# Strassen's seven quarter products for the second matrix product of an attention and feed-forward kernel

## The chip, the cores and the metric

The kernel runs on one core of a Trainium2 chip. The metric is the time of the program on the device in microseconds; the median of three runs of the kernel before is 319.86 us (319.72 to 320.0). The profile is of one execution, with a span of 317.4 us from its first to its last instruction.

The engines are named as in the profile: PE is TensorE (its weight loads are PEld), DVE is VectorE, ACT is ScalarE, POOL is GpSimd, SP is SyncE, which issues the stores. Each works through its own instructions in the order of the program.

## The reference, cut to what matters

```python
# q, k, v: (8 batches, 8 heads, 576 tokens, 64) float32; g_norm: (64,)
kv  = einsum('bhsd,bhse->bhde', k, v)
out = einsum('bhsd,bhde->bhse', q, kv)
rms = sqrt(mean(out * out, axis=-1, keepdims=True) + 1e-06)
out = out / rms * g_norm

x = out.transpose(0, 2, 1, 3).reshape(4608, 512)
h = x @ w_in                                  # w_in (512, 2048)
g = maximum(h, 0) + alpha * minimum(h, 0)     # alpha (2048,)
y = g @ w_out                                 # w_out (2048, 512), result float32
```

Linear attention without a softmax, a norm for each head, and a feed-forward part of two matrix products with a leaky activation between them.

## The kernel before

The 4608 tokens are worked on in nine blocks of W = 512 columns, numbered 0 to 8. For a block w the kernel makes `xt` (the normed attention output, features on the partitions), then 16 groups of the first product, `h_ps`, each 128 of the 2048 inner features by 512 tokens; each group leaves PSUM through ScalarE and VectorE as a tile `gt`. The second product takes `gt` as stationary operand, 128 tokens at a time, and sums 16 matmuls into a bank `y`.

```python
def ssq_mm(w, j):                       # norm of a pair of heads
    ot_ps, sq = ots.pop((w, j))
    ssq_ps = ps_q.tile([P, W], FP32, name="ssq_ps", tag="q")
    nc.tensor.matmul(out=ssq_ps[:], lhsT=mask16[:], rhs=sq[:], start=True, stop=True)
    rstd = attn_p.tile([P, W], FP32, name="rstd")
    nc.scalar.activation(out=rstd[:], in_=ssq_ps[:], func=AF.Ln, bias=eps_t[:], scale=inv_d)
    nc.scalar.activation(out=rstd[:], in_=rstd[:], func=AF.Exp, bias=0.0, scale=-0.5)
    ...
def m1_mm(h_ps, w, g, cs):              # first product: 4 matmuls of 512 columns a group
    for c in cs:
        nc.tensor.matmul(out=h_ps[:], lhsT=w_in_blk(c, g), rhs=xts[w, c][:], ...)

def m1_evac(h_ps, w, g):
    m_sb = gt_p.tile([P, W], FP32, name="m_sb", bufs=3)
    nc.scalar.activation(out=m_sb[:], in_=h_ps[:], func=AF.Relu, scale=-1.0)
    gt = gt_p.tile([P, W], FP16, name="gt", tag=f"gt{g}")
    nc.vector.scalar_tensor_tensor(out=gt[:], in0=m_sb[:], scalar=beta_sb[:, g : g + 1],
                                   in1=h_ps[:], op0=ALU.mult, op1=ALU.add)

def y_mm(y, w, a, g):                   # second product: 64 matmuls of 512 columns a block
    nc.tensor.matmul(out=y[:], lhsT=gts[w, g][:, a * P : (a + 1) * P], rhs=w_out_blk(g), ...)
```

The inputs of a batch (576 tokens) are loaded through Pool's queue and, for k and q, regrouped by a copy on Pool. The stage buffers are double.

```python
def load_batch(b, names=("k", "v", "q")):
    for nm in names:
        load_rem(b, nm)                 # nc.gpsimd.dma_start
        load_main(b, nm, 0, H)          # nc.gpsimd.dma_start into a stage tile (2 buffers)

def regroup_batch(b):
    for nm in ("k", "q"):
        regroup(b, nm, 0, H, nc.gpsimd) # a copy on Pool of 128x2048
```

The main loop runs the first product of block w together with the second product of block w - 1, and between the groups the attention steps of block w + 1 (`t` transposes q, `kv` makes k times v, `ot` multiplies both, `ssq` makes the norm and `xt`). The steps `t` and `kv` write one PSUM bank, `ssq` another.

```python
for w in range(1, NW):
    steps = window_steps(w + 1) if w + 1 < NW else []
    if 1 < w and w + 2 < B:
        load_batch(w + 2)
        regroup_batch(w + 2)
    for g in range(NF):                 # 16 groups
        if w == 1 and g == first_g - 1:
            load_batch(3)
            regroup_batch(3)
        m1_group(w, g)
        if w == 1:                      # the last quarter of block 0's second product
            y_mm(y, 0, AHEAD, g) ...
        else:                           # four matmuls of block w - 1's second product
            for gg in range(part * TPW, (part + 1) * TPW):
                y_mm(y, w - 1, a, gg)
            ...
        while steps and n - len(steps) < want:
            steps.pop(0)()
for a in range(TPW):                    # block 8's second product, with nothing beside it
    ...
```

PSUM has eight banks: three for `h_ps`, one for `y`, one for `t` and `kv`, two for `ot`, one for `ssq`.

Of the kernel before, what the change touches and what calls it, by code (L numbers as in the profile page):

```python
# [9 lines left out]
FP32 = mybir.dt.float32  # L10
FP16 = mybir.dt.float16
AF = mybir.ActivationFunctionType
# [5 lines left out]
def kernel(  # L18
# [11 lines left out]
    nc = tc.nc  # L30

    B, H, S, D = q.shape
    N_TOK, D_MODEL = out.shape
    D_FF = moe_w_in.shape[1]

    P = 128
    NPAIR = H // 2
    W = 512
    NW = N_TOK // W
    TPW = W // P  # L40
    TPP = S // P
    MAIN = TPP * P
    REM = S - MAIN
    NT = TPP + 1
    NF = D_FF // P
    NC = D_MODEL // P
    assert NC == NPAIR and 0 < REM < P
    inv_d = 1.0 / D

    const_p = ctx.enter_context(tc.tile_pool(name="constp", bufs=1))  # L50
    w_p = ctx.enter_context(tc.tile_pool(name="weights", bufs=1))
    xt_p = ctx.enter_context(tc.tile_pool(name="xt", bufs=3))
    qkv_p = ctx.enter_context(tc.tile_pool(name="qkv", bufs=1))
    stage_p = ctx.enter_context(tc.tile_pool(name="stage", bufs=2))
    attn_p = ctx.enter_context(tc.tile_pool(name="attn", bufs=2))
    gt_p = ctx.enter_context(tc.tile_pool(name="gt", bufs=2))
    ysb_p = ctx.enter_context(tc.tile_pool(name="ysb", bufs=4))
    ps_h = ctx.enter_context(tc.tile_pool(name="psh", bufs=3, space=bass.MemoryType.PSUM))
    ps_y = ctx.enter_context(tc.tile_pool(name="psy", bufs=1, space=bass.MemoryType.PSUM))
    ps_s = ctx.enter_context(tc.tile_pool(name="pss", bufs=1, space=bass.MemoryType.PSUM))  # L60
    ps_o = ctx.enter_context(tc.tile_pool(name="pso", bufs=2, space=bass.MemoryType.PSUM))
    ps_q = ctx.enter_context(tc.tile_pool(name="psq", bufs=1, space=bass.MemoryType.PSUM))
# [3 lines left out]
    )  # L66

    _set_id = list(get_activation_tables(nc.m.arch).keys()).index(
        "natural_log_exp_and_others"
    )  # L70
    nc.scalar.add_instruction(
        mybir.InstLoadActFuncSet(
            name=nc.get_next_instruction_name(),
# [18 lines left out]
    eps_t = const_p.tile([P, 1], FP32, name="eps_t")  # L92
# [5 lines left out]
    for nm, src in (("q", q), ("k", k), ("v", v)):  # L98
        rem0[nm] = ysb_p.tile([P, H, D], FP32, name=f"rem0{nm}", tag="y_sb")
        nc.sync.dma_start(  # L100
            out=rem0[nm][0:REM], in_=src[0, :, MAIN:S, :].rearrange("h s d -> s h d"),
# [12 lines left out]
    bufs = []  # L114
    for i in range(NBUF):
        t = {}
        for nm in ("k", "v", "q"):
            n = 1 if nm == "v" else NT
# [39 lines left out]
    WQ = 4  # L158
    w_in_sb = []
    w_out_sb = []  # L160
    FW = D_FF // WQ
    GW = NF // WQ
# [21 lines left out]
    def w_out_blk(g):  # L184
        i, r = divmod(g, GW)
        return w_out_sb[i][:, r, :]
# [14 lines left out]
    def keep_warm(n):  # L201
        ps = ps_s.tile([P, W], FP32, name="warm_ps", tag="s")
        for i in range(n):
            nc.tensor.matmul(out=ps[:], lhsT=mask16[:], rhs=warm16[:], start=True, stop=True)
# [4 lines left out]
        out=alpha_ps[:], lhsT=alpha_row[:], rhs=ident[0:NF, 0:NF], is_transpose=True,  # L209
        start=True, stop=True,  # L210
    )

    beta_sb = const_p.tile([P, NF], FP32, name="beta_sb")
    nc.vector.tensor_scalar(
        out=beta_sb[:], in0=alpha_ps[:], scalar1=-1.0, scalar2=1.0, op0=ALU.mult, op1=ALU.add,
# [42 lines left out]


    ots = {}  # L260

    def step_ot(w, j, pool=None):
        if pool is not None:
            ot_ps = pool[0].tile([P, W], FP32, name="ot_ps", tag=pool[1])
        else:
            ot_ps = ps_o.tile([P, W], FP32, name="ot_ps", tag="o")
        n0 = w * W
        while n0 < (w + 1) * W:
            b = n0 // S
            n1 = min((b + 1) * S, (w + 1) * W)  # L270
            nc.tensor.matmul(  # L271
                out=ot_ps[:, n0 - w * W : n1 - w * W], lhsT=kvs[b, j][:],
                rhs=qts[b, j][:, n0 - b * S : n1 - b * S], start=True, stop=True,
            )
            n0 = n1
        sq = attn_p.tile([P, W], FP16, name="sq_sb")
        nc.scalar.activation(out=sq[:], in_=ot_ps[:], func=AF.Square)  # L277
        ots[w, j] = (ot_ps, sq)
# [4 lines left out]

    def ssq_mm(w, j):
        ot_ps, sq = ots.pop((w, j))
        ssq_ps = ps_q.tile([P, W], FP32, name="ssq_ps", tag="q")
        nc.tensor.matmul(out=ssq_ps[:], lhsT=mask16[:], rhs=sq[:], start=True, stop=True)  # L287
        rstd = attn_p.tile([P, W], FP32, name="rstd")
        nc.scalar.activation(  # L289
            out=rstd[:], in_=ssq_ps[:], func=AF.Ln, bias=eps_t[:], scale=inv_d,  # L290
        )
        nc.scalar.activation(out=rstd[:], in_=rstd[:], func=AF.Exp, bias=0.0, scale=-0.5)  # L292
        ots[w, j] = (ot_ps, rstd)

    def norm(w, j):
# [21 lines left out]


    gts = {}

    def m1_mm(h_ps, w, g, cs):
        for c in cs:
            nc.tensor.matmul(  # L323
                out=h_ps[:], lhsT=w_in_blk(c, g), rhs=xts[w, c][:],
                start=(c == 0), stop=(c == NC - 1),
            )

    def m1_evac(h_ps, w, g):
        m_sb = gt_p.tile([P, W], FP32, name="m_sb", bufs=3)
        nc.scalar.activation(out=m_sb[:], in_=h_ps[:], func=AF.Relu, scale=-1.0)  # L330
        gt = gt_p.tile([P, W], FP16, name="gt", tag=f"gt{g}")
        nc.vector.scalar_tensor_tensor(  # L332
            out=gt[:], in0=m_sb[:], scalar=beta_sb[:, g : g + 1], in1=h_ps[:],
            op0=ALU.mult, op1=ALU.add,
        )
        gts[w, g] = gt

    def m1_group(w, g):
        h_ps = ps_h.tile([P, W], FP32, name="h_ps", tag="h")
        m1_mm(h_ps, w, g, range(NC))  # L340
        m1_evac(h_ps, w, g)


    def y_mm(y, w, a, g):
        nc.tensor.matmul(  # L345
            out=y[:], lhsT=gts[w, g][:, a * P : (a + 1) * P], rhs=w_out_blk(g),
            start=(g == 0), stop=(g == NF - 1),
        )

    def y_out(y, w, a):  # L350
        y_sb = ysb_p.tile([P, D_MODEL], FP32, name="y_sb")
        nc.scalar.copy(out=y_sb[:], in_=y[:])  # L352
        i = 0
        while i < P:
            b, r = divmod(w * W + a * P + i, S)
            if r < MAIN:
                t, p = divmod(r, P)
                cnt = min(P - i, P - p)
                rows = out[b * S : b * S + MAIN, :].rearrange("(p t) m -> t p m", t=TPP)
                dst = rows[t, p : p + cnt, :]  # L360
            else:
                cnt = min(P - i, S - r)
                dst = out[b * S + r : b * S + r + cnt, :]
            nc.sync.dma_start(out=dst, in_=y_sb[i : i + cnt, :])
            i += cnt


    H_POOL = (ps_h, "h")
    for nm in ("q", "k", "v"):
        nc.scalar.copy(out=bufs[0][nm][0:REM, 0 if nm == "v" else TPP, :, :], in_=rem0[nm][0:REM])  # L370
    regroup(0, "q", 0, H // 2)
    step_t(0, 0, H_POOL)
    regroup(0, "k", 0, H // 2)
    step_t(0, 1, H_POOL)
    keep_warm(3)
    step_kv(0, 0)
    step_kv(0, 1, H_POOL)
    step_ot(0, 0)
    step_ot(0, 1)
    regroup(0, "q", H // 2, H)  # L380
    step_t(0, 2, H_POOL)
    regroup(0, "k", H // 2, H)
    step_t(0, 3, H_POOL)
    ssq_mm(0, 0)
    ssq_mm(0, 1)
    norm(0, 0)
    step_kv(0, 2)
    step_kv(0, 3, H_POOL)
    norm(0, 1)
    step_ot(0, 2)  # L390
    step_ot(0, 3, (ps_y, "y"))
    first = [ps_h.tile([P, W], FP32, name="h_ps", tag="h") for g in range(3)]
    for g in range(3):
        m1_mm(first[g], 0, g, (0, 1))
    step_ssq(0, 2)
# [7 lines left out]
    for g in range(3, NF):  # L403
# [7 lines left out]
    AHEAD = 3  # L411
    ys = [
        ps_y.tile([P, W], FP32, name="ya", tag="y"),
        ps_h.tile([P, W], FP32, name="yb", tag="h"),
        ps_h.tile([P, W], FP32, name="yc", tag="h"),
    ]
    steps = window_steps(1)
    n = len(steps)
# [6 lines left out]
        y_out(ys[a], 0, a)  # L425
    regroup_batch(2)

    for w in range(1, NW):
        steps = window_steps(w + 1) if w + 1 < NW else []
        n = len(steps)  # L430
        first_g = 4 if w == 1 else 0
        if 1 < w and w + 2 < B:
            load_batch(w + 2)
            regroup_batch(w + 2)
        y = None
        for g in range(NF):
            if w == 1 and g == first_g - 1:
                load_batch(3)
                regroup_batch(3)
            m1_group(w, g)  # L440
            if w == 1:
                if g == 0:
                    y = ps_y.tile([P, W], FP32, name="y_ps", tag="y")
                y_mm(y, 0, AHEAD, g)
                if g == NF - 1:
                    y_out(y, 0, AHEAD)
            else:
                a, part = divmod(g, TPW)
                if part == 0:
                    y = ps_y.tile([P, W], FP32, name="y_ps", tag="y")  # L450
                for gg in range(part * TPW, (part + 1) * TPW):
                    y_mm(y, w - 1, a, gg)
                if part == TPW - 1:
                    y_out(y, w - 1, a)

            want = n * (g - first_g + 1) // (NF - 2 - first_g)
            while steps and n - len(steps) < want:
                steps.pop(0)()
    for a in range(TPW):
        y = ps_h.tile([P, W], FP32, name="y_ps", tag="h")  # L460
        for g in range(NF):
            y_mm(y, NW - 1, a, g)
        y_out(y, NW - 1, a)


# [28 lines left out]
```

## Time and profile before

| Quantity | Value |
|---|---|
| Time, median of three | 319.86 us |
| Span of the profiled execution | 317.4 us |
| PE busy | 293.4 us (92%), 1588 matmuls |
| DVE busy | 157.2 us (50%) |
| ACT busy | 173.4 us (55%) |
| POOL busy | 66.6 us (21%) |
| Mean granted TensorE clock | 0.993 |
| Chain that ended last | PE 85%, ACT 6%, DVE 4%, DMA 2% |

A busy time is the sum of the durations of an engine's instructions where they don't overlap. A matmul's duration holds its latency, and matmuls follow one another before the last has ended, so the rate of PE is read from the distance of their starts. In the rows of the costliest groups, "busy, mean ns" is followed by the time in which the engine stood idle just before such an instruction, and by what ended that. In a timeline a bracket at the end of a line gives the idle time before the instruction and the one that released it. In a list of waits the three numbers are the total in us, how often, and the longest.

### The profile page before, as it was taken

How to read it: one execution, taken by the hardware profiler on the slowest of the kernel's cores; microseconds unless marked ns; L12 is line 12 of the kernel's file. 1: busy time of each engine (PE TensorE's matmuls, PEld its weight loads, DVE VectorE, ACT ScalarE, POOL GpSimd, SP SyncE). 2: the span in 40 equal slices, each digit the busy share in tenths (PEclk: the TensorE clock that was granted, in tenths of full speed). 3: DMA queues.
4: the chain of work that ended last, by engine and by line, in shares of the span. 5: the costliest groups of instructions: out<-in, count | busy, mean ns of one | idle time of the engine just before them, and what ended most of it. 6: DMA issues, size and time to landing. Idle time of an engine off the chain costs nothing.

```text
span 317.4 us, 4195 instructions
## 1 busy us (share of the span) xinstructions
PE 293.4 (92%) x1588; PEld 142.0 (45%) x1588; DVE 157.2 (50%) x267; ACT 173.4 (55%) x292; POOL 66.6 (21%) x74
## 2 busy tenths in 40 slices
PE   5668998898999999999999999999999999999994
PEld 1323453454455455545554455444544444444441
DVE  4547833666655554545464546454554445443300
ACT  2366546468466636674567456655665667444211
POOL 8434312737340541055005200000000000000000
PEclk9799999999999999999999999999999999999999
DMA  7999999998973859077715811000011111001132
GB/s 110 179 206 195 200 197 143 174 149 89 169 101 51 115 92 118 34 104 113 108 35 86 120 35 33 33 36 33 33 35 33 33 33 36 33 34 37 52 80 66
DMA packets 47621, 28.27 MB, mean 89 GB/s; under 512 B 14304, under 2 KB 42992, under 8 KB 47600
## 3 DMA queue, kind: packets, MB, share of 16 engines
q0 software_dynamic: 40320, 18.16, 45.7%
q1 hardware_dynamic: 7280, 9.84, 11.2%
q8 instruction: 12, 0.20, 0.3%
q14 instruction: 9, 0.07, 0.1%
HBM read 36.71 MB, written 9.44 MB: 145 GB/s over the span
## 4 chain that ended last, share of the span: by engine, by line
PE 85%; ACT 6%; DVE 4%; DMA 2%; issue 1%; SPq 1%; ACTq 0%
PE h_ps L323 37%; PE y_ps L345 36%; PE qt_ps L234 3%; PE kv_ps L249 3%; PE ssq_ps L287 3%; PE ot_ps L271 2%; DMA alpha_row<-in_moe_alpha_dram 2%; ACT rstd L289 2%; ACT sq_sb L277 1%; ACT rstd L292 1%; DVE gt L332 1%; DVE xt L298 1%; ACT m_sb L330 1%; SPq L100 1%; PE yb L345 1%
## 5 line engine op out<-in xcount | busy, mean ns | idle before, releaser
L332 DVE SCALAR_TENSOR_TENSOR gt<-m_sb,beta_sb,h_ps 128x512 f16<-128x512 f32 x144 | 106.8, 745 | 87.2 <-ACT m_sb L330 86.4
L323 PE MATMUL h_ps<-xt,w_in_sb 128*128 128x512 f16 x576 | 146.2, 379 | 2.9 <-DVE xt L298 1.7
L345 PE MATMUL y_ps<-w_out_sb,gt 128*128 128x512 f16 x528 | 134.8, 379 | 0.1
L330 ACT ACTIVATE m_sb<-h_ps 128x512 f32<-128x512 f32 x144 | 85.3, 594 | 80.4 <-PE h_ps L323 80.3
L345 PEld LDWEIGHTS <-gt 128*128 128x128 f16 x576 | 56.1, 98 | 67.1 <-issue 1.7
L323 PEld LDWEIGHTS <-w_in_sb 128*128 128x128 f16 x576 | 54.2, 98 | 64.2 <-issue 10.4
L298 DVE SCALAR_TENSOR_TENSOR xt<-ot_ps,g2col,rstd 128x512 f16<-128x512 f32 x36 | 27.0, 751 | 43.3 <-ACT rstd L292 43.2
L289 ACT ACTIVATE rstd<-ssq_ps,eps_t 128x512 f32<-128x512 f32 x36 | 24.7, 687 | 18.0 <-PE ssq_ps L287 17.9
L277 ACT ACTIVATE sq_sb<-ot_ps 128x512 f16<-128x512 f32 x36 | 21.3, 596 | 16.2 <-PE ot_ps L271 15.6
L352 ACT COPY y_sb<-y_ps 128x512 f32<-128x512 f32 x33 | 19.3, 586 | 18.4 <-PE y_ps L345 18.4
L292 ACT ACTIVATE rstd<-rstd 128x512 f32<-128x512 f32 x36 | 22.7, 629 | 1.1
L287 PE MATMUL ssq_ps<-sq_sb,mask 128*128 128x512 f16 x36 | 13.6, 378 | 6.7 <-ACT sq_sb L277 5.6
L129 POOL DMA_DIRECT2D vst<-in_v_dram x9 | 7.7, 860 | 50.4 <-PE kv_ps L249 48.6
L146 POOL COPY qsb<-qst 128x2048 f16<-128x2048 f16 x6 | 11.4, 1897 | 32.5 <-DMA qst<-in_q_dram 32.5
L249 PEld LDWEIGHTS <-ksb 128*128 128x128 f16 x160 | 11.6, 99 | 11.2 <-issue 4.2
L234 PE MATMUL qt_ps<-ident,qsb 128*128 128x128 f16 x160 | 14.4, 225 | 1.9 <-DVE qsb L146 1.2
L234 PEld LDWEIGHTS <-qsb 128*128 128x128 f16 x160 | 11.6, 101 | 9.4 <-DVE qsb L146 2.4
L243 DVE COPY qt_sb<-qt_ps 128x576 f16<-128x576 f16 x32 | 14.4, 451 | 2.5 <-PE qt_ps L234 2.5
L271 PE MATMUL ot_ps<-qt_sb,kv_sb 128*128 128x512 f16 (+7 forms) x64 | 13.5, 286 | 0.8 <-DVE kv_sb L257 0.7
L249 PE MATMUL kv_ps<-vst,ksb 128*128 128x128 f16 x128 | 12.3, 220 | 1.8 <-DVE qt_sb L243 1.8
L146 POOL COPY ksb<-kst 128x2048 f16<-128x2048 f16 x6 | 11.4, 1903 | 11.9 <-DMA kst<-in_k_dram 11.9
L257 DVE TENSOR_TENSOR kv_sb<-kv_ps,mask 128x128 f16<-128x128 f32 x32 | 9.0, 285 | 3.8 <-PE kv_ps L249 3.8
(43 smaller groups left out, 92.6 us busy)
## 6 DMA issues: line engine op xcount, KB each, us to landing
out_dram<-y_sb SPq DMA_DIRECT2D x40, 128.0 KB, 2.4
out_dram<-y_sb SPq DMA_DIRECT2D x16, 256.0 KB, 2.3
kst<-in_k_dram POOLq DMA_DIRECT2D x7, 512.0 KB, 6.9
qst<-in_q_dram POOLq DMA_DIRECT2D x7, 512.0 KB, 10.1
vst<-in_v_dram POOLq DMA_DIRECT2D x7, 512.0 KB, 8.4
w_in_sb<-in_moe_w_in_dram POOLq DMA_DIRECT2D x4, 512.0 KB, 14.7
w_out_sb<-in_moe_w_out_dram POOLq DMA_DIRECT2D x4, 512.0 KB, 16.1
qst<-in_q_dram POOLq DMA_DIRECT2D x2, 256.0 KB, 7.5
```

The costliest lines, as they stand in the source:

```text
L146: (eng or nc.vector).tensor_copy(out=dst, in_=src)
L234: nc.tensor.matmul(out=qt_ps[:, t * P : (t + 1) * P], lhsT=qs(t), rhs=ident16[:], is_transpose=True, start=(t == 0), stop=(t == NT - 1),)
L249: nc.tensor.matmul(out=kv_ps[:], lhsT=ks(t), rhs=vs(t), start=(t == 0), stop=(t == NT - 1),)
L277: nc.scalar.activation(out=sq[:], in_=ot_ps[:], func=AF.Square)
L287: nc.tensor.matmul(out=ssq_ps[:], lhsT=mask16[:], rhs=sq[:], start=True, stop=True)
L289: nc.scalar.activation(out=rstd[:], in_=ssq_ps[:], func=AF.Ln, bias=eps_t[:], scale=inv_d,)
L292: nc.scalar.activation(out=rstd[:], in_=rstd[:], func=AF.Exp, bias=0.0, scale=-0.5)
L298: nc.vector.scalar_tensor_tensor(out=xts[w, j][:], in0=ot_ps[:], scalar=g2col[:], in1=rstd[:], op0=ALU.mult, op1=ALU.mult,)
L323: nc.tensor.matmul(out=h_ps[:], lhsT=w_in_blk(c, g), rhs=xts[w, c][:], start=(c == 0), stop=(c == NC - 1),)
L330: nc.scalar.activation(out=m_sb[:], in_=h_ps[:], func=AF.Relu, scale=-1.0)
L332: nc.vector.scalar_tensor_tensor(out=gt[:], in0=m_sb[:], scalar=beta_sb[:, g : g + 1], in1=h_ps[:], op0=ALU.mult, op1=ALU.add,)
L345: nc.tensor.matmul(out=y[:], lhsT=gts[w, g][:, a * P : (a + 1) * P], rhs=w_out_blk(g), start=(g == 0), stop=(g == NF - 1),)
```

## The change

For blocks 1 to 8, `g` (512 tokens by 2048) is cut into four quarters A11, A12 (tokens 0 to 255) and A21, A22 (tokens 256 to 511), each with half of the inner features, and `w_out` into B11, B12, B21, B22, each 1024 by 256. Seven products of quarters take the place of eight, in the form of Strassen's method that has few sums:

- sums of g: S1 = A21 + A22 and S2 = S1 - A11 on VectorE; S3 = A11 - A21 and S4 = A12 - S2 on Pool; fp16, each in four parts of 128x512 for a block
- sums of w_out: once, eight operations of 128x1024 on VectorE after block 1
- a product is 16 matmuls of 256 columns; products 1 and 2 go to bank X, 6, 7 and 4 to Y, 5 and 3 to Z, and the banks are read between products, two reads on ScalarE and five additions on VectorE for a block

To have a bank for Y, the first product keeps two banks from block 2 on; Z takes the bank of `ssq`, and `ssq` goes into the bank of `t` and `kv`. The order of the first product's groups is changed so that the halves for a sum are ready together. The inverse root becomes one function of ScalarE, with the function table that holds it. The stores of a block become quarters with rows of 256 columns. It is meant to lower the number of columns that TensorE streams. The diff, cut to its core:

```diff
-        nc.scalar.activation(
-            out=rstd[:], in_=ssq_ps[:], func=AF.Ln, bias=eps_t[:], scale=inv_d,
-        )
-        nc.scalar.activation(out=rstd[:], in_=rstd[:], func=AF.Exp, bias=0.0, scale=-0.5)
+        nc.scalar.activation(
+            out=rstd[:], in_=ssq_ps[:], func=AF.Abs_reciprocal_sqrt, bias=eps_t[:], scale=inv_d,
+        )
...
+    def w_sums(i):                      # i in 0, 1: four operations of 128x1024
+        nc.vector.tensor_sub(out=t1, in0=w_lo(i, HC, D_MODEL), in1=w_lo(i, 0, HC))
+        nc.vector.tensor_sub(out=t2, in0=w_hi(i, HC, D_MODEL), in1=t1)
+        nc.vector.tensor_sub(out=t4, in0=w_hi(i, 0, HC), in1=t2)
+        nc.vector.tensor_sub(out=w_lo(i, HC, D_MODEL), in0=w_hi(i, HC, D_MODEL), in1=w_lo(i, HC, D_MODEL))
...
+    def s_sum(w, n, k):                 # k = 0 to 3: a quarter of the inner features of a half
+        if n == 1:
+            nc.vector.tensor_add(out=t[:], in0=a21, in1=a22)
+        elif n == 2:
+            nc.vector.tensor_sub(out=t[:], in0=sums[w, 1, k][:], in1=a11)
+        elif n == 3:
+            nc.gpsimd.tensor_sub(out=t[:], in0=a11, in1=a21)
+        else:
+            nc.gpsimd.tensor_sub(out=t[:], in0=a12, in1=sums[w, 2, k][:])
...
+    Y_ORDER = (1, 6, 2, 7, 5, 4, 3)     # 7 x 16 matmuls, 7 in each of the 16 units of a block
+    Y_READS = {2: ("p1",), 5: ("u2",), 7: ("c11",), 9: ("u3",), 12: ("c22",), 14: ("c21",)}
+    G_ORDER = [0, 1, 8, 9, 2, 3, 10, 11, 4, 5, 12, 13, 6, 7, 14, 15]
...
+    def unit_sums(w, u):
+        k, r = divmod(u, 4)
+        k -= 1
+        if k >= 0 and r < 2:
+            s_sum(w, 1 if r == 0 else 2, k)
+            s_sum(w, 3 if r == 0 else 4, k)
...
+        if w == 2:
+            h_tags[0] = ("h0", "h1")
+            ssq_pool[0] = (ps_s, "s")
         if 1 < w and w + 2 < B:
             load_batch(w + 2)
             regroup_batch(w + 2)
...
+            m1_group(w, G_ORDER[u])
+            unit_sums(w, u)
+            if w > 1 and u < 2:
+                unit_sums(w - 1, NF + u)        # the last quarter of the block before
+            if w > 2 and u == 0:
+                y_read(w - 2, "c12")
...
+                for i in range(u * PER, (u + 1) * PER):
+                    prod_mm(w - 1, *Y_LIST[i])
+                for what in Y_READS.get(u, ()):
+                    y_read(w - 1, what)
```

The reads are: p1 (X after product 1, on ScalarE), u2 (Y + p1 after product 6), c11 (X after product 2, on ScalarE), u3 (Y + p1 after product 7), c22 (Z + u3 after product 5), c21 (Y + p1 after product 4) and c12 (Z + u2 after product 3).

## The prediction, made before the result was known

> **What bounds the kernel now.** I read the page first, then the chain that ended last, then TensorE's waits, and at the end the timelines of a steady token block and of Pool. In the slices of the span TensorE is the full row, at full clock, while Pool has work only in the first half:
>
> ```profile
> PE   5668998898999999999999999999999999999994
> ...
> POOL 8434312737340541055005200000000000000000
> PEclk9799999999999999999999999999999999999999
> ```
>
> The chain gives PE 85% of the span. TensorE's busy time counts latency too (379 ns each for the two products), so the rate must come from the distance between starts. In the chain, groups of four 512-column matmuls touch end to end:
>
> ```profile
> 207.80 0.86 PE h_ps L323 x4
> 208.66 0.86 PE y_ps L345 x4
> 209.53 0.86 PE h_ps L323 x4
> ```
>
> Four take 0.863 us, so **216 ns each**. The same pattern comes back from 191.22 to 223.66: a full block takes **32.44 us**. Counting: 128 product matmuls at 216 ns are 27.65; transposes and kv products are eight groups of five 128-column matmuls; ot and ssq are 8 x 512 columns, 1.75. The groups of five show what small matmuls cost:
>
> ```profile
> 81.32 0.44 PE L234 MATMUL qt_ps<-ident,qsb 128*128 128x128 f16 x5
> 81.60 1.03 PE L323 MATMUL h_ps<-xt,w_in_sb 128*128 128x512 f16 x4
> ```
>
> Five in 0.28 us, 56 ns each, weight loads hidden; eight groups are 2.24. The sum is 31.64, and the remaining 0.8 is one wait per block:
>
> ```profile
> PE ssq_ps L287 <- ACT sq_sb L277: 5.6, 7, 1.1
> PE kv_ps L249 <- DVE qt_sb L243: 1.8, 4, 0.6
> ```
>
> So TensorE's columns are the bound, and removing columns pays as long as nobody else becomes late. VectorE's main row and Pool's copies are:
>
> ```profile
> L332 DVE SCALAR_TENSOR_TENSOR gt<-m_sb,beta_sb,h_ps 128x512 f16<-128x512 f32 x144 | 106.8, 745 | 87.2 <-ACT m_sb L330 86.4
> ...
> L146 POOL COPY qsb<-qst 128x2048 f16<-128x2048 f16 x6 | 11.4, 1897 | 32.5 <-DMA qst<-in_q_dram 32.5
> ```
>
> Last, Pool in order of time around the start of block 2 (79.35 us) and block 3:
>
> ```profile
> 72.53 0.69 POOL L135 DMA_DIRECT2D ksb<-in_k_dram  x1
> ...
> 76.30 0.92 POOL L129 DMA_DIRECT2D qst<-in_q_dram  x1
> 79.72 1.90 POOL L146 COPY ksb<-kst 128x2048 f16<-128x2048 f16 x1 [2.50 <-DMA kst<-in_k_dram]
> 86.62 1.90 POOL L146 COPY qsb<-qst 128x2048 f16<-128x2048 f16 x1 [5.00 <-DMA qst<-in_q_dram]
> ...
> 104.04 0.89 POOL L129 DMA_DIRECT2D vst<-in_v_dram  x1 [13.33 <-PE kv_ps L249]
> ```
>
> Pool is one queue in program order: loading batch 3 and regrouping it occupies the queue from 72.53 to 88.52, **16.0 us**, of which most is waiting for data, and nothing behind it can run. Today nothing behind it is urgent. That is the row to remember.
>
> [...] No tensor_tensor of this shape is in the trace; its fp16 copies (417 ns for 1024, 685 for 2048) show a fixed part of 149 ns. With half that copy rate, 512 elements are an estimated 0.42 us and 1024 are 0.69. [...] the granted clock is below full only in the first slices.
>
> **The change part by part.**
>
> *Columns.* A block's second product goes from 64 x 216 ns = 13.82 us to 112 matmuls of 256 columns. Between 56 ns for 128 and 216 for 512 a straight line gives 109 ns, so 12.23. Saved: **1.6 us per block, 12.7 us in eight blocks**. This is the whole prize.
>
> *VectorE in a steady block.* Now 16 x 0.745 + 4 x 0.751 + 4 x 0.451 + 4 x 0.285 = 17.9 us. Added: eight sums x 0.42 and five bank reads x about 0.70 (the gt operation's tile, one operand fewer) = 6.9. Together 24.8 of some 31 us: not the bound, but bursty. I followed the queue unit by unit (a unit is one first-product group with seven quarter matmuls, 1.63 us, plus a 0.2 to 0.3 step). After a group's matmuls the gt value is finished 2.45 us after the unit's start, and consecutive VectorE operations overlap by about 0.08. In unit 0 it then has a sum, the c12 read and the qt copy, to about 3.75, while kv wants the bank at 3.54: with the signal, some 0.25 lost. The u2 read before product 7 loses about 0.05 and the c22 read before product 3 about 0.2. Sum: 0.5 us of new waits. A first-product bank is held 2.5 us and comes round every 3.3 to 3.8, so **two banks suffice** on average. A steady block becomes 32.44 - 1.6 + 0.5 = **31.4**.
>
> *Inverse root.* One function instead of two removes 629 ns x 36 from ScalarE, which isn't the bound. At the start, however, the chain between 11 and 26 us holds three of these Exp (0.63, 0.64, 0.64 us). I take 1.5 us gained there.
>
> *Block 1.* It has few matmuls per unit; VectorE gets six sums, 2.5 us. I allow 0.7 lost. Block 2 then starts at 79.35 - 1.5 + 0.7 = 78.5.
>
> *Weight sums.* Eight operations of 1024 elements, 8 x 0.69 less overlaps = 5 us, enter VectorE's queue just before block 2[...]. TensorE runs out of banks after two units: some 5 us late.
>
> *Pool's order: the main term.* Sums 3 and 4 of block 1's last quarter are issued in block 2's units 0 and 1, **behind** the loads and copies of batch 4. The first six Pool sums of block 1 are themselves behind the copies of batch 3, which end at 88.5. So: 88.5 + 6 x 1.2 = 95.7; load and regroup of batch 4 at the 16.0 us measured for batch 3: 111.7; sum 3 of the last quarter: 112.9. Product 7 wants it at matmul 54 of 112, in unit 7, which is 15.6 us into the block by my unit count: 78.5 + 5 + 15.6 = 99. TensorE stands still for about **14 us**, and the weight sums' delay vanishes inside this wait rather than adding to it. [...]
>
> In blocks 3 to 5 the same order holds, but the loads start earlier relative to the block: Pool is free after sum 4 of the third quarter, about 1.6 us before the block's start; plus 16.0 plus 1.2 is 15.6, exactly when it is wanted. I allow 0.5 each. From block 6 on there are no loads.
>
> *Sum.* 113.0 (sum 3 seen) + 15.8 (rest of block 2) + 1.7 = 130.5; three blocks at 31.9: 226.2; block 6 at 31.4 and block 7 at 29.2 (it prepares only 512 tokens without transposes and kv, 2.24 less): 286.8; block 8 without steps, 27.65 - 1.6 + 0.6: 313.5; the last products 12.4, a last read 0.75, and from there to the end 4.0 as before plus some 0.8 for the twice as many stores: 331.5. The timed figure was 2.5 above the span: 334. As my constants for Pool are more likely high than low, I say **333**.
>
> **Rivals.** *A: the gain arrives.* If Pool's sums were never waited for, then 319.9 - 12.7 + 4 (steady waits) - 1.5 + 5 gives about 315. For it: reads are placed one or two units after their products, which leaves them slack. Against it: Pool's order above, and the 16 us measured. *B: VectorE or the two banks become the bound.* At 24.8 of 31 us with sums excluded by Pool copies, each block could lose 2 us instead of 0.5, for about 345 with the Pool wait. Against it: the mean load is 80%, and only 1.3 us separates bank hold and return. *C: the wait is there but shorter.* Pool sums of 0.6 us would move the release seven times 0.6 earlier and empty the 0.5 waits: about 327.
>
> **Range and chances.** The Pool wait follows from program order and a measured load time, so I hold it 85% likely; its size moves by about 4 us with the duration of Pool's sums, and the steady blocks by 5 either way. Hence 325 to 341. Slower by over 2% begins at 326.3.
>
> **What would show it.** Right: in TensorE's waits, product matmuls waiting for a Pool subtraction, one of 10 us or more near 100 to 113 us; Pool's timeline with batch 4's q copy directly before it; 256-column matmuls 109 ns apart; steady blocks of 31 to 32 us. Wrong: no such wait, Pool subtractions under 0.6 us, or gt values that return late and make first-product matmuls wait in every block. What would upset it most is a 256-column matmul paced by its weight load, or functions outside the loaded table.

## The result, and the profile after

The changed kernel takes **323.94 us** (median of four runs, 323.46 to 324.88) against 319.79 us for the kernel before on the same chip: ratio 1.0141, 95% interval 1.012 to 1.0163. It is 1.4% slower. The prediction was 333 us, with 325 to 341 as its range.

The page of the changed kernel, in its 40 slices:

```profile
PE   5678899898499999899979997999999999999990
...
POOL 8424313749645272937274726622222223432400
PEclk9799999999899999999999999999999999999997
```

TensorE is no longer a full row. Counted from 0, it has a hole in slice 10 (80 to 88 us) and weaker slices, 16, 20 and 24, where Pool shows high digits; the clock has one new dip in mid-run, in slice 10 too. TensorE's waits name what the holes are (in total, how often, the longest):

```profile
PE kv_ps L251 <- DVE qt_sb L245: 5.6, 3, 4.6
PE yY L460 <- POOL s L421: 4.9, 3, 2.0
PE ssq_ps L290 <- ACT sq_sb L280: 4.5, 7, 0.7
```

The third is the old wait of the norm. The first two are new: one of 4.6 us behind the weight sums, and three for Pool's sum 3. The groups of the costliest instructions give the size of what was added to Pool, here for sum 4 (sum 3 has 1174 ns):

```profile
L423 POOL TENSOR_TENSOR s<-gt,s 128x512 f16<-128x512 f16 x32 | 37.4, 1170 | 90.1 <-DVE s L419 50.1
```

In the chain of the last products, "1.75 PE yX L460 x16" is 109.4 ns for a matmul of 256 columns.

With marks at the last norm matmul of each block (the same matmul in both programs) the span divides like this:

| Stretch, us | Before | After | Difference |
|---|---|---|---|
| start to the mark in block 1 | 76.98 | 74.99 | -2.0 |
| to the mark in block 2 | 31.39 | 37.32 | +5.9 |
| blocks 3 to 5 | 97.33 | 99.49 | +2.2 |
| block 6, without loads | 32.44 | 31.35 | -1.1 |
| block 7 | 29.35 | 28.01 | -1.3 |
| to the last matmul | 45.3 | 42.6 | -2.7 |
| last matmul to the end | 4.6 | 7.6 | +3.0 |
| span | 317.4 | 321.4 | +4.0 |

Where nothing but the products' columns and the reads count, the change gains. It loses in block 2, wherever Pool loads, and behind the last matmul. Each has a cause of its own. TensorE in block 2:

```profile
80.47 0.93 PE L460 MATMUL yX<-w_out_sb,gt 128*128 128x256 f16 x7
86.03 0.58 PE L251 MATMUL kv_ps<-vst,ksb 128*128 128x128 f16 x4 [4.64 <-DVE qt_sb L245]
86.41 0.31 PE L251 MATMUL kv_ps<-vsb,ksb 128*128 128x128 f16 x1
86.52 1.91 PE L332 MATMUL h_ps<-xt,w_in_sb 128*128 128x512 f16 x4
```

After the wait the four matmuls of the first product take 1.91 us from first start to last end, not 1.03: the granted clock is 0.50 from 85.3 to 88.7 us. And Pool before block 5's sum 3, with TensorE's wait for it:

```profile
179.82 0.71 POOL L137 DMA_DIRECT2D ksb<-in_k_dram  x1
...
187.22 1.89 POOL L148 COPY ksb<-kst 128x2048 f16<-128x2048 f16 x1 [2.67 <-DMA kst<-in_k_dram]
196.02 1.89 POOL L148 COPY qsb<-qst 128x2048 f16<-128x2048 f16 x1 [6.91 <-DMA qst<-in_q_dram]
197.88 1.15 POOL L421 TENSOR_TENSOR s<-gt 128x512 f16<-128x512 f16 x1
...
199.08 0.39 PE L460 MATMUL yY<-w_out_sb,s 128*128 128x256 f16 x2 [2.01 <-POOL s L421]
```

The sum ends at 199.03 and TensorE resumes at 199.08 after a wait of 2.01 us. The sum's inputs had been ready since the block before; it stood behind a load that nobody wanted yet.

The last stretch is the stores. In the trace's answer for `y_sb`, from 290 us on:

```profile
L374 SPq DMA_DIRECT2D out_dram<-y_sb x24: 332/594/597, 297.8 to 317.9; - x24
...
L485 DVE TENSOR_TENSOR y_sb<-yZ,u x2: 684/688/692, 302.5 to 313.8; 128x512 f32<-128x512 f32 x2
```

The last read ends at 314.5, but its last store is issued at 317.9. Block 8's four quarters are sixteen stores of mostly 0.59 us in one issuing queue. The first quarter's four are out by 309.8; the other twelve follow without a gap from 311.0 to 318.5, 7.5 us of issuing for three quarters that are read within 3.5 us.

### The profile page after: what moved, and what is told of

Same layout as the page of the kernel before. It is cut to its first block, busy times and chain, and to the rows that moved or that the text cites. A ratio compares the mean times of both kernels' runs of the same rounds, so it can differ in the third digit from the quotient of the medians.

```text
span 321.4 us, 5167 instructions
## 1 busy us (share of the span) xinstructions
PE 285.7 (89%) x1972; PEld 179.7 (56%) x1972; DVE 211.2 (66%) x379; ACT 144.4 (45%) x240; POOL 140.1 (44%) x138
## 4 chain that ended last, share of the span: by engine, by line
PE 56%; DMA 10%; issue 10%; DVE 9%; POOL 9%; ACT 4%; POOLq 0%; DVEq 0%; ACTq 0%
PE h_ps L332 26%; PE yY L460 10%; PE yZ L460 7%; DMA kst<-in_k_dram 6%; DMA w_in_sb<-in_moe_w_in_dram 4%; PE yX L460 4%; DVE gt L343 3%; ACT m_sb L339 2%; PE ssq_ps L290 2%; POOL qsb L148 2%; POOL ksb L148 2%; PE kv_ps L251 2%; PE ot_ps L274 2%; POOL s L423 1%; POOL s L421 1%
## 5 line engine op out<-in xcount | busy, mean ns | idle before, releaser
L423 POOL TENSOR_TENSOR s<-gt,s 128x512 f16<-128x512 f16 x32 | 37.4, 1170 | 90.1 <-DVE s L419 50.1
L460 PEld LDWEIGHTS <-s 128*128 128x128 f16 x512 | 49.9, 98 | 26.5 <-POOL s L421 5.8
L460 PEld LDWEIGHTS <-gt 128*128 128x128 f16 x384 | 37.6, 98 | 15.2 <-issue 0.6
L421 POOL TENSOR_TENSOR s<-gt 128x512 f16<-128x512 f16 x32 | 37.6, 1174 | 0.0
L460 PE MATMUL yX<-w_out_sb,gt 128*128 128x256 f16 x256 | 35.4, 274 | 0.0
L300 DVE SCALAR_TENSOR_TENSOR xt<-ot_ps,g2col,rstd 128x512 f16<-128x512 f32 x36 | 26.9, 746 | 12.9 <-ACT rstd L292 12.8
L292 ACT ACTIVATE rstd<-ssq_ps,eps_t 128x512 f32<-128x512 f32 x36 | 24.7, 687 | 17.5 <-PE ssq_ps L290 17.3
L460 PE MATMUL yY<-w_out_sb,s 128*128 128x256 f16 x128 | 19.2, 273 | 5.0 <-POOL s L421 4.9
L251 PE MATMUL kv_ps<-vst,ksb 128*128 128x128 f16 x128 | 12.7, 225 | 6.0 <-DVE qt_sb L245 5.6
L460 PE MATMUL yZ<-w_out_sb,s 128*128 128x256 f16 x128 | 17.5, 272 | 0.3 <-DVE y_sb L483 0.2
L460 PE MATMUL yY<-wsum,s 128*128 128x256 f16 x128 | 17.6, 273 | 0.0
L460 PE MATMUL yZ<-wsum,s 128*128 128x256 f16 x128 | 17.6, 273 | 0.0
L460 PE MATMUL yY<-wsum,gt 128*128 128x256 f16 x128 | 17.6, 273 | 0.0
```

The source lines that it names most:

```text
L251: nc.tensor.matmul(out=kv_ps[:], lhsT=ks(t), rhs=vs(t), start=(t == 0), stop=(t == NT - 1),)
L292: nc.scalar.activation(out=rstd[:], in_=ssq_ps[:], func=AF.Abs_reciprocal_sqrt, bias=eps_t[:], scale=inv_d,)
L300: nc.vector.scalar_tensor_tensor(out=xts[w, j][:], in0=ot_ps[:], scalar=g2col[:], in1=rstd[:], op0=ALU.mult, op1=ALU.mult,)
L421: nc.gpsimd.tensor_sub(out=t[:], in0=a11, in1=a21)
L423: nc.gpsimd.tensor_sub(out=t[:], in0=a12, in1=sums[w, 2, k][:])
L460: nc.tensor.matmul(out=bank[:, a, :], lhsT=lhs, rhs=rhs, start=fresh, stop=(i == 2 * NK - 1), skip_group_check=True,)
```

## The experiments

Each ratio is to the kernel before, run on the same chip in the same job.

### Pool's sums ahead of the loads

```diff
-        if 1 < w and w + 2 < B:
-            load_batch(w + 2); regroup_batch(w + 2)
...
                 unit_sums(w - 1, NF + u)
+            if 1 < w and w + 2 < B and u == 1:
+                load_batch(w + 2); regroup_batch(w + 2)
```

> Changed kernel, with the loads and copies of batch w + 2 issued on Pool after the last two Pool sums of block w - 1 instead of before them (blocks 2 to 5). Theory (Pool's program order makes product 7 wait): the three waits of 1.1, 1.8 and 2.0 us for the Pool sum disappear and blocks 3 to 5 fall from 33.2 to about 31.4 us, so about 5 us less, 319. Rival (it is the exclusion of VectorE sums by Pool work, or the landing of the data, that costs): the waits stay or turn up at VectorE's sums and the time stays within 1 us of 324.

320.92 us, 1.0017 (0.999 to 1.0045). No wait for a Pool sum is left in the list of waits. Blocks 3, 4 and 5, measured between the first matmuls of their product 1, are 31.7, 31.6 and 32.3 us instead of 32.7, 33.3 and 33.5. So Pool's order is what held product 7. The gain is 3 us by the medians (4.0 by the ratios) and not 5, for two reasons that the lists show: the wait behind the weight sums grew from 4.6 to 6.3, and product 3 now waits for the c22 read (2.5 us in five waits). The first comes from the rival's exclusion: Pool's sums now run beside the weight sums. So do the two long ones of the second (0.93 and 0.96): the sum 1 ahead of the read runs beside a Pool sum there and takes 1.33 and 1.36 us instead of 0.42. VectorE's timeline at the weight sums:

```profile
80.08 1.52 DVE L401 TENSOR_TENSOR wsum<-w_out_sb,wsum 128x1024 f16<-128x1024 f16 x1
81.63 1.52 DVE L402 TENSOR_TENSOR wsum<-w_out_sb,wsum 128x1024 f16<-128x1024 f16 x1
83.08 0.68 DVE L403 TENSOR_TENSOR w_out_sb<-w_out_sb,w_out_sb 128x1024 f16<-128x1024 f16 x1
```

and Pool's at the same time:

```profile
79.46 1.60 POOL L423 TENSOR_TENSOR s<-gt,s 128x512 f16<-128x512 f16 x1
81.01 1.60 POOL L421 TENSOR_TENSOR s<-gt 128x512 f16<-128x512 f16 x1
```

Both are longer than alone (0.68 and 1.15), and they go in step.

### The weight sums spread

The six sums that don't overwrite `w_out` go into block 0's second product, where VectorE has room; the two in place go into block 2.

```diff
-                    for i in range(2):
-                        w_sums(i)                  # after block 1: eight in a row
+        if 9 <= g < 15:                            # in block 0's second product
+            w_sums(*divmod(g - 9, 3))              # one of six
...
+            if w == 2 and u in (2, 3):
+                w_sums(u - 2, 3)                   # one in place
```

> Changed kernel, with six of the eight weight sums issued during block 0's second product, one in each of six groups, and the two in place in units 2 and 3 of block 2. Theory (eight sums in a row hold VectorE's queue, TensorE stands 4.6 us and then runs at half clock for a few matmuls): block 2 falls from 38.1 us by 6 to 32, time about 318; but sum 3 of block 1 will then be wanted earlier, and if Pool's order matters a new wait of about 3 us for it appears in block 2, which would leave only some 3 us, 321. Rival (block 2 is long for other reasons): under 1.5 us.

322.06 us, 1.0064 (1.0013 to 1.0115). The 4.6 us wait is gone and block 2 takes 34.5 us instead of 38.1, and as expected sum 3 is wanted earlier: 2.88 us of waiting for it appear in block 2, and the waits for Pool go from 4.9 in three to 8.0 in four. One loss had been hiding another.

```profile
96.45 0.39 PE L464 MATMUL yY<-w_out_sb,s 128*128 128x256 f16 x2 [2.88 <-POOL s L425]
```

### The last stores from two queues

```diff
+            turn[0] += 1
+            eng = nc.scalar if n0 >= (NW - 1) * W and turn[0] % 2 else nc.sync
-            nc.sync.dma_start(out=dst, in_=src[i : i + cnt])
+            eng.dma_start(out=dst, in_=src[i : i + cnt])
```

> Changed kernel, with every other store of the last block issued from ScalarE's queue instead of SyncE's. Theory (20 stores of 0.6 us each pile up in one issuing queue behind the last products): the 7.6 us between the last matmul and the end fall to about 5, time 321.4. Rival (the stores land late because rows of 256 columns are slow to write): no change beyond 0.5 us.

321.76 us, 1.0059 (1.0026 to 1.0091). From the last matmul to the end it is now 5.1 us instead of 7.6 (316.0 to 321.1), with sixteen stores in the last block, not the twenty that I had counted. The rows of 256 columns as such are not slow to land (2.0 to 2.1 us from issue to landing, in the median, in the changed kernel; rows of 512 in the kernel before took 2.3 to 2.4); the issuing was.

### All three

> The three moves together. Theory: they are separate losses and add: 323.9 - 5 - 6 - 2.5 gives about 310.5, faster than the kernel before by about 3%, with blocks 2 to 6 all near 31.4 us. Rival (VectorE's load or the two banks for the first product is what costs): the waits move to gt values and the time stays above 316.

**309.84 us**, 0.9679 (0.9645 to 0.9712). Alone the three gave 3.0, 1.9 and 2.2 us by the medians, together 14.1 (by the ratios 4.0, 2.5, 2.6 and 14.8), since the first had lengthened the wait behind the weight sums and the second had uncovered one for Pool; the runs show no such part for the stores. Blocks 2 to 6 are 31.9, 31.4, 31.7, 32.2 and 31.4 us, the mean clock is 1.000, and TensorE's waits hold only one new entry of size, product 3 for the c22 read:

```profile
PE yZ L468 <- DVE y_sb L491: 2.3, 4, 0.9
```

### Parts of the change alone

> Kernel before, with the inverse root as one function and nothing else. Theory: only the chain at the start is shortened, 1.5 to 2 us, so 318.2, with blocks 2 to 6 unchanged at 32.44 us. Rival (ScalarE's 629 ns per pair matters in each block too): 315 or less.

316.01 us, 0.9882 (0.9853 to 0.991): 3.7 us gained, with 2.9 to 4.7 in the interval. Blocks 3 to 6 stay at 32.44, so the gain is at the start, as in the theory, but more of it: in the profile the stretch from the last norm matmul for block 0 to the last for block 1 shrinks from 31.52 to 29.68 us, and the next, which is block 1 with its short units, where the norm's chain counts, from 24.53 to 23.45. The two make 2.9 us. The rival is out for the steady blocks. I had left out block 1.

> Kernel before, with two banks for the first product from block 2 on and the norm's sums in the bank of the transposes, without quarter products. Theory: a bank is held 2.5 us and comes round every 3.5, so nothing changes, 319.9 within 0.5 us. Rival (two banks are too few): first-product matmuls wait for gt values and each block grows by 1 us or more, 326.

320.11 us, 1.0009 (0.9981 to 1.0036). Blocks 3 to 6 are 32.44 us as before. Two banks for the first product, and the norm in the transposes' bank, cost nothing that these runs can measure. The change also has two buffers instead of three for `xt` and `m_sb`, and another order of groups. These were not run alone; TensorE's waits for `xt` are 0.8 us in the changed kernel where they were 1.7.

### All sums on VectorE

In the version with all three moves, sums 3 and 4 are issued on VectorE too.

> The version with all three moves, with sums 3 and 4 on VectorE as well. It adds 8 x 0.42 us, so VectorE has about 28 of 31.4 us in a block. If VectorE's load is what limits, blocks grow by 1 to 2 us, 317 to 322. If there is room, the end of the exclusion between VectorE's sums and Pool's work gives back what the additions cost: 309 to 312.

331.66 us, 1.0354 (1.0282 to 1.0427), far above both; it is the median of three runs (329.06 to 333.34), and a fourth, of 336.46 us with a lower granted clock than theirs, is left out. Against the version it came from, the profiled span is 21.5 us longer: 5.4 before block 2, 4.4 in block 2, 8.8 in blocks 3 to 5, and 2.9 from block 6 on. What the additions alone cost is seen in block 6, where Pool has no copies: 31.36 us become 32.47, the amount that I had expected everywhere. In blocks 2 to 4 something else is added. Each time a sum 1 meets a Pool copy of k and lasts 2.68, 2.68 and 3.12 us instead of 0.42:

```profile
109.36 2.68 DVE L425 TENSOR_TENSOR s<-gt 128x512 f16<-128x512 f16 x1
...
109.83 1.92 POOL L148 COPY ksb<-kst 128x2048 f16<-128x2048 f16 x1
```

The c22 read stands behind that sum, product 3 waited 2.6, 2.6 and 3.0 us for it. In block 2 half clock followed, with four matmuls of the first product in 1.91 us from 114.69, and the mean clock of the run is 0.983, against 1.000 with all three moves. In block 1, with its short units, VectorE was busy for 7.1 of the last 7.6 us even without them. Three times the 1.1 us of block 6 is 3.3, so some 9.6 of the 12.9 us lost in blocks 2 to 4 come from VectorE's exclusion by Pool's copies and from what followed it, not from VectorE's load. With the copies on Pool and this order of VectorE's queue, the two sums are better left on Pool; with the reads moved ahead of the sums it was not tested.

### More work on Pool

The first adds a second copy of k in blocks 3 to 5, in the changed kernel as it was.

> Changed kernel as it was, with the copy of k on Pool done twice for the batches loaded in blocks 3 to 5. Theory (Pool's order in front of sum 3 sets these blocks): the copy takes 1.89 us, the waits of 1.1, 1.8 and 2.0 us become about 3, 3.7 and 3.9 if q has landed by then; where q's landing is what ends last, the second copy of k lies beside it and costs nothing. Since the k copy is over 6 us before the q copy begins, I expect the second case: no change, within 0.5 us of 323.9. A rise of 5 to 6 us would mean that the queue's work and not the landing sets the release.

324.46 us, 1.0146 (1.0107 to 1.0186): no change, the waits for Pool 5.4 instead of 4.9 us. The k copies run as a pair of 3.84 us from 121.60, and the q copy starts at 129.69 (129.19 in the changed kernel), when q lands. What sets the release is the order plus q's landing, not the amount of Pool's work.

The second tests the state that the prediction assumed, with Pool a batch behind. Eight spare copies follow the copies of batch 3:

```diff
                 regroup_batch(3)
+                for _ in range(8):      # into batch 4's buffer, free here and written again later
+                    nc.gpsimd.tensor_copy(out=bufs[1]["k"]..., in_=stages[3, "k"][:])
```

> Changed kernel as it was, with eight spare copies of 1.89 us on Pool in block 1 behind the copies of batch 3 (into a buffer that is free and is written again later), so that Pool is about one batch, 15 us, later at block 2. This is the state that the prediction took for the real one. If its account of Pool's order holds, sum 3 of block 1's last quarter ends near 111 to 112 instead of 96.6, TensorE waits 11 to 13 us for it in block 2, runs cold for a while after, and the time is 336 to 338. Rival (the sums' lateness is partly absorbed elsewhere): below 332.

342.06 us, 1.0722 (1.0655 to 1.0788). The time is 4 us above the range expected, and the mechanism isn't the one expected: the wait behind the weight sums was 14.2 us and the one for Pool in block 2 only 2.8, at 114.57. The spare copies were still running and held the weight sums off, one by one:

```profile
80.88 2.26 DVE L401 TENSOR_TENSOR wsum<-w_out_sb,wsum 128x1024 f16<-128x1024 f16 x1
83.18 2.26 DVE L402 TENSOR_TENSOR wsum<-w_out_sb,wsum 128x1024 f16<-128x1024 f16 x1
```

A weight sum of 0.69 us took 2.26, about the length of a stretched copy. So the same copies were set behind the version with spread weight sums:

> The version with the weight sums spread, with the eight spare copies on Pool in block 1. In the run with the spare copies alone the copies and the weight sums held each other up on VectorE's side, so it didn't show the wait by itself. Here the weight sums are out of the way. Theory: six sums end near 95, batch 4 is loaded and copied by 111, sum 3 by 112; TensorE wants it at 93.5, so one wait of 17 to 19 us for Pool, a cold clock after it, and 337 to 340. Rival: TensorE is again held before that point by VectorE, and the wait for Pool stays under 5 us.

341.27 us, 1.0664 (1.0618 to 1.0711), 1 us above the range expected. TensorE and Pool:

```profile
94.68 0.71 PE L464 MATMUL yY<-w_out_sb,s 128*128 128x256 f16 x5
114.24 0.61 PE L464 MATMUL yY<-w_out_sb,s 128*128 128x256 f16 x2 [18.86 <-POOL s L425]
```

```profile
95.73 0.71 POOL L137 DMA_DIRECT2D ksb<-in_k_dram  x1
...
111.18 1.90 POOL L148 COPY qsb<-qst 128x2048 f16<-128x2048 f16 x1 [4.42 <-DMA qst<-in_q_dram]
113.04 1.15 POOL L425 TENSOR_TENSOR s<-gt 128x512 f16<-128x512 f16 x1
```

One wait of 18.86 us, before the sixth of the unit's seven matmuls, released when sum 3 ends at 114.2. The predicted release was 112.9. The granted clock stays at 0.50 until 117.8, 3.6 us behind the wait, which makes a loss of 1.8.

### VectorE's order, and the norm

Two more versions build on the one with all three moves. In the first, the u2 and c22 reads go ahead of their unit's sum and the c12 read moves one unit on:

```diff
+            if w > 1 and u in (5, 12):
+                for what in Y_READS[u]:
+                    y_read(w - 1, what)
             unit_sums(w, u)
...
-            if w > 2 and u == 0:
+            if w > 2 and u == 1:
                 y_read(w - 2, "c12")
```

> The version with all three moves and only the change of VectorE's order (u2 and c22 reads ahead of the unit's sum, c12 read one unit later). Theory: 309.8 - 2.3 - 1.5, about 306. Rival: VectorE's order only moves the waits to the sums' users, 309 to 310.

305.47 us, 0.9558 (0.9516 to 0.96). No read is waited for any longer; blocks 3 to 6 take 30.95, 31.44, 31.08 and 30.95.

In the second, besides, the last norm of a block is issued one unit after its product:

```diff
+            if u == NF - 3:
+                want = n - 1
             while steps and n - len(steps) < want:
                 steps.pop(0)()
```

> The version with all three moves, and in VectorE's queue the u2 and c22 reads ahead of the unit's sum, the c12 read one unit later, and the last norm of a block one unit after the product it needs. Theory: the waits of product 3 for c22 (2.3 us in four blocks), of kv for the qt copy (some 0.25 a block) and of the norm's matmul for the square (0.65 a block, 4.5 in all) go, 309.8 - 2.3 - 1.5 - 4.5 gives 302 to 304. Rival: the xt of the last pair comes so late that the next block's first group waits for it, 307 or more.

**300.59 us**, 0.9397 (0.9362 to 0.9432), 6% faster than the kernel before and below the 302 to 304 expected. The wait for the square falls from 4.5 us to 0.4, and blocks 3 to 6 are 30.10 us each. My count for a block without any wait was 31.64 - 1.6 = 30.04.

## Why the prediction was wrong

**The step that failed is "Pool's order: the main term"**, and in it one reading: I took the copies at 79.72 and 86.62 for batch 3's. They are batch 4's. There are six pairs of copies, for batches 2 to 7, and counting them from the first pair (48.39 and 55.09, which is batch 2) puts batch 3 at 64.52 and 70.69. In the changed kernel Pool passed from batch 3's q copy straight to block 1's sums:

```profile
70.42 1.90 POOL L148 COPY qsb<-qst 128x2048 f16<-128x2048 f16 x1 [4.74 <-DMA qst<-in_q_dram]
72.28 1.15 POOL L421 TENSOR_TENSOR s<-gt 128x512 f16<-128x512 f16 x1
...
93.41 1.89 POOL L148 COPY qsb<-qst 128x2048 f16<-128x2048 f16 x1 [4.28 <-DMA qst<-in_q_dram]
95.27 1.32 POOL L421 TENSOR_TENSOR s<-gt 128x512 f16<-128x512 f16 x1
```

Sum 3 of block 1's last quarter was done at 96.6, not 112.9; the difference of 16.3 is one load and regroup. TensorE came for it at 99.6, near the 99 of the prediction, and found it ready. The mechanism was right: with Pool made a batch late, the wait appeared in full (18.86 us). It was one batch off in time.

**The consequence for the next step:** "the weight sums' delay vanishes inside this wait" fell with it. The delay, taken as some 5 us, showed as a wait of 4.64 plus half clock to 88.7, so block 2, from its first first-product matmul to that of block 3, took 38.1 us (77.70 to 115.77) where I had summed 52.0 (78.5 to 130.5). These 13.9 us are the error of the prediction; smaller ones the other way leave the predicted span of 331.5 ten too long.

**Terms that were mis-sized.** Blocks 3 to 5: I allowed 0.5 us for Pool in each and they had 1.1, 1.8 and 2.0, since a load with its copies took 17.3 to 18.1 us there, not the 16.0 read from one batch; together they were 3.8 above the sum. Block 7 took 28.0 where I had 29.2. The end: 0.8 for twice as many stores was some 3, because the stores of the quarters before the last one are still queued when it is read. The inverse root: 1.5 was 3.7 when alone, with block 1 left out. In the changed kernel part of that goes to block 1's sums: block 2 began at 77.70 where I had 78.5.

**What held.** Three figures of the prediction were assumptions of mine that no trace of before shows: half the rate of the fp16 copies for VectorE's sums, 1.2 us for a sum on Pool, and the 1.7 us in its total for a clock at half after the wait. Columns: 109 ns estimated, 109.4 found. Sums on VectorE 0.42 us assumed, 0.42 found alone and 0.438 to 0.494 in the mean, with those beside Pool's work in it; weight sums 0.69 and 0.68 to 0.69 (one of 1.27 beside a Pool sum); Pool's sums 1.2 and 1.17; the clock 1.7 and 1.8 (with the spare copies and the weight sums spread); reads 0.70 and 0.685. A steady block 31.4 and 31.35, with the small waits in it: the kv matmuls of block 6 start 0.26 late where I had 0.25, and moving the reads took such a block from 31.36 to 30.95, 0.4 where I had 0.5 in all. Two banks suffice. Rival A, the gain arriving at about 315, came only when the three moves were made together (309.84); rival B, VectorE as the bound, did not show in the changed kernel, but the exclusion that it named made a sum of 0.42 us last 2.68 to 3.12 beside a Pool copy, and waits of 2.6 to 3.0 us, in three blocks of the version with all sums on VectorE; rival C, a shorter wait of Pool with 327, came nearest, but for another reason than faster Pool sums.

The change as it was given is slower because its 12.7 us of columns and 2 us at the start meet about 19 us of new losses: 7 to 8 in block 2, 5 of Pool's order, 3 of stores, and the rest in small VectorE waits. The first three are read from the traces, and removing them together gave 14.1 us of their 15 to 16. The last is what remains; moving VectorE's reads gave back some 4 (309.84 to 305.47 us).

## What to carry to other kernels

When a queue takes on work that others wait for, look at what stands ahead of it in program order: a load with its wait is worth its whole latency to everything behind it, here 17.3 to 18.1 us with the copies. Before you use a row of a trace for a given pass of a loop, count the passes from the first one. And add up losses only after removing them together: here three moves gave 3.0, 1.9 and 2.2 us alone, by the medians, and 14.1 together.

## What the runs showed of the hardware

**Half clock after a wait of 2.24 us.** The granted clock by stretch, in the run with two store queues, around a 2.24 us wait for Pool that ended at 166.46 (columns: length, busy times of PE, PEld, DVE, ACT and POOL, then the clock, DMA share and GB/s):

```profile
166.00:167.00 1.00, 0.54 (x5) 0.48 (x6) 0.00 (x0) 0.00 (x0) 1.00 (x2) 0.83 0.33 85
167.00:168.00 1.00, 1.00 (x7) 0.56 (x5) 0.29 (x1) 0.00 (x0) 1.00 (x2) 0.50 0.23 59
...
169.00:170.00 1.00, 1.00 (x6) 0.73 (x5) 0.16 (x1) 0.60 (x1) 1.00 (x2) 0.50 0.00 0
170.00:171.00 1.00, 1.00 (x8) 0.59 (x6) 1.00 (x2) 0.31 (x1) 0.86 (x1) 0.97 0.00 0
```

Half clock lasted about 3.4 us, and block 4 took 35.4 us instead of the changed kernel's 33.3. The longer wait is 0.5 of that; half of 3.4 is another 1.7.

The length of the wait alone does not decide. After one of 2.17 us (the run with the k copy twice, ending at 199.85) four matmuls of the first product took 1.91 us from 200.38, half clock again. After one of 2.88 us (the run with the weight sums spread, ending at 96.45) the same four took 1.03, and after the 2.01 us in block 5 of the changed kernel the clock was 1.00. What the trace of the changed kernel shows besides is when the clock fell to 0.50: at 10.17, 85.26 and 317.37 us. The first two times at half lasted 3.413 us each, and the falls are 75.09 and 232.11 us apart, 22 and 68 times that. How this and the length of a wait together decide was not shown.

**VectorE's sums and Pool's work took turns.** In the run with the spare copies a weight sum of 0.69 us took 2.26 beside Pool copies that took 2.23 instead of 1.90, and in the run with Pool's sums ahead of the loads 1.52 beside Pool sums of 1.60 instead of 1.15. The gt operations, which read `h_ps` from PSUM, took 0.75 us beside the same copies (at 77.75 and 78.83), as in their mean. I had not expected that each side would get one instruction at a time: with the spare copies, weight sums start at 80.88, 83.18, 85.36 and 87.65, and the three copies from 82.66 on take 6.82 us together, one of each in some 2.3 us, 0.3 less than the two take alone.
